# Expert products of 512 columns that walk their operands 16 bytes in every 64, in four passes

## The chip, the core and the metric

The kernel runs on one core of one Trainium2 chip. The metric is the time of one execution on the device in microseconds (us). Five engines work side by side: TensorE (PE, matrix products; its loads of stationary weights have rows of their own, PEld), VectorE (DVE), ScalarE (ACT), GpSimd (POOL) and SyncE (SP), which issues the DMAs.

## The reference

A linear attention with a decaying state runs over 4 batches, 8 heads, 768 tokens and 48 channels; its output, laid out as 3072 tokens by 384, goes through one expert (two matrix products with a gate between them):

```
for t in range(S):                       # attention, per batch and head
    cur = outer(u * k[t], v[t])
    y[t] = r[t] @ (state + cur)
    state = w[t][:, None] * state + outer(k[t], v[t])
h = x @ w_in                             # x: 3072 x 384, w_in: 384 x 2048
g = where(h >= 1, h, where(h <= -1, 0, (h + 1) ** 2 / 4))
out = g @ w_out                          # w_out: 2048 x 384
```

All of it is fp32. The expert's products are made of three terms each, high part by high part, high by low and low by high, in the 32-bit format float32r.

## The kernel before

**Tiling.** The 3072 tokens are cut into 6 blocks of 512 (`WIDE`), and the hidden width 2048 into 16 chunks `f` of 128. A *step* is one block and one chunk, and consists of `product_in`, the gate, and `product_out`:

- `product_in` makes `h` (128 hidden units by 512 tokens, one PSUM bank) out of 9 matmuls: 3 pieces `j` of the 384 inputs by 3 terms. Weights are the stationary operand (`wt`), tokens the moving one (`x`), 512 columns each.
- The gate: ACT `Relu` (L755) and `Square` (L756), DVE minimum and maximum (L757), ACT rounding to `gh` (L759), DVE remainder `gl` (L760).
- `product_out` adds into three PSUM banks `acc` with 9 matmuls, moving operand `gh` (six) or `gl` (three), 512 columns each. It runs up to two or three steps behind `product_in` (`LAG`); `h` has two buffers, `g`, `gh` and `gl` have three.

In block 0 the first 5 chunks and in block 1 the first 11 are done for each half of the block apart (`HALVES`), with 256 columns per matmul; so there are 32 half steps and 80 whole ones, 2016 expert matmuls in all, 1440 of them with 512 columns.

**Attention.** Twelve units of 256 tokens, two for each block, make the next blocks' `x` while a block runs: small matmuls (48 or 64 columns, in quarter tiles of the array: `among`, `umat`, `cross`, `along`), transposes, scans on DVE, copies on ACT. The weights arrive and are decoded during block 0. `zeros` and `warm` put matmuls on cleared data (L326) into PE's gaps in the first part.

**Order.** All operations are put into a `Plan`, which simulates the engines with the costs written beside each operation and writes out a fixed order for every engine. The order is emitted as it stands; the tile framework adds the waits on semaphores from the regions that each instruction reads and writes.

Of the kernel before, what the change touches and what calls it, by code (L numbers as in the profile page):

```python
# [32 lines left out]
WIDE = 2 * UT  # L33
# [201 lines left out]
def attention_moe(tc, a):  # L235
# [501 lines left out]
    def products(n):  # L737
# [8 lines left out]
        for half in range(2):  # L746
# [4 lines left out]
        step_ops.append(len(plan.ops))  # L751
        op("PE", 0.16 + 2.11 * k, due, [("wh", f), ("wl", f), *xs], [("b", 6 + hk)],
           lambda: product_in(nc, hs, f, x[:, 0, :, cs], x[:, 1, :, cs], w_hi, w_lo))
        c = 0.21 + 0.40 * k
        op("ACT", c, due, [("b", 6 + hk)], [("g", gk)], lambda: nc.scalar.activation(gs, hs, AF.Relu, scale=0.5, bias=0.5))  # L755
# [10 lines left out]
        for terms in LAST if done else [TERMS]:  # L766
            op("PE", 0.16 + 2.11 * k * len(terms) / 9, due, [("gh", gk), ("gl", gk), ("wh", f), ("wl", f)],
               sorted({("b", 3 + j) for _, j in terms}), fresh=begin,
               emit=lambda terms=terms: product_out(nc, [x[:, cs] for x in acc], f, ghs, gls, w_hi, w_lo, begin, end, terms))
# [64 lines left out]
def general(tc, a, ident, w_hi, w_lo):  # L834
# [65 lines left out]
    with (  # L900
# [3 lines left out]
        with tc.For_i(0, B, 1) as b:  # L904
            for third in range(UB):
                ts = slice(third * UT, third * UT + UT)
                x = sb.tile([128, 3, UT], F32, tag="x", name=f"gx{third}")
                for h in range(2):
                    for j in range(3):
                        nc.sync.dma_start(  # L910
                            out=x[64 * h : 64 * h + D, j, :],
                            in_=xd[bass.ds(b, 1), j // 2 * 2 + h, j % 2 * 64 : j % 2 * 64 + D, ts],
                        )
                        nc.sync.dma_start(
                            out=x[64 * h + D : 64 * h + 64, j, :],
                            in_=xd[bass.ds(b, 1), 2 + h, 64 + 16 * j : 80 + 16 * j, ts],
                        )
                xh = sb.tile([128, 3, UT], F32R, tag="xh", name=f"gxh{third}")
                xl = sb.tile([128, 3, UT], F32R, tag="xl", name=f"gxl{third}")
                A.copy(xh, x)  # L920
                G.tensor_tensor(out=xl, in0=x, in1=xh.bitcast(F32), op=ALU.subtract)
                o = [ps.tile([128, UT], F32, tag=f"o{j}", name=f"go{third}{j}") for j in range(3)]
                for f in range(NF):
                    hp = ps.tile([128, UT], F32, tag="h", name=f"gh{third}_{f}")
                    product_in(nc, hp, f, xh, xl, w_hi, w_lo)
                    gh, gl = gate(nc, sb, hp, f"g{third}_{f}")
                    product_out(nc, o, f, gh, gl, w_hi, w_lo, f == 0, f == NF - 1)
                for j in range(3):
                    ob = sb.tile([128, UT], F32, tag=f"ob{j}", name=f"gob{third}{j}")
                    A.copy(ob, o[j])  # L930
                    for c2 in range(2):
                        nc.sync.dma_start(out=a["out_b"][bass.ds(b, 1), third, j, :, c2], in_=ob[:, c2 * 128 : c2 * 128 + 128].rearrange("p (g s) -> p g s", g=2))


def product_in(nc, hp, f, xh, xl, w_hi, w_lo):
    n = 0
    for j in (2, 0, 1):
        cs = slice(j * 128, j * 128 + 128)
        for wx, xt in ((w_hi, xh), (w_hi, xl), (w_lo, xh)):
            nc.tensor.matmul(hp, lhsT=wx[f][:, cs], rhs=xt[:, j, :], start=n == 0, stop=n == 8)  # L940
            n += 1


# [11 lines left out]
def product_out(nc, o, f, gh, gl, w_hi, w_lo, first, stop, terms=None):  # L955
    parts = ((gh, w_hi), (gh, w_lo), (gl, w_hi))
    for i, j in terms or [(i, j) for i in range(3) for j in range(3)]:
        gt, wx = parts[i]
        cs = slice(384 + j * 128, 384 + j * 128 + 128)
        nc.tensor.matmul(  # L960
            o[j], lhsT=wx[f][:, cs], rhs=gt, start=first and i == 0, stop=stop and i == 2, skip_group_check=True
        )


# [65 lines left out]
```

## Time and profile before

| | |
|---|---|
| time, median of 3 runs | 519.95 us (519.9 to 522.65) |
| profiled execution: its span, first to last instruction | 518.1 us |
| what lies around the span, by the median | 1.85 us |
| PE busy | 501.7 us, 97% |
| PE weight loads busy (beside PE) | 413.4 us, 80% |
| DVE, ACT, POOL busy | 333.6, 296.1 and 101.0 us |
| expert matmuls, share of the chain that ended last | 69% (L940 35%, L960 34%) |
| granted TensorE clock, mean | 0.998 |

No time of the profiled execution is recorded besides its span; the median of the runs is taken for it. A matmul's record is longer than the distance between two matmuls, because they are pipelined and their ends are modelled: what a matmul costs is read from the distance between starts, not from its duration. Two times that differ by less than 0.5% (2.6 us) can't be told apart.

### The profile page before, as it was taken

Reading aid. Unit: us, or ns where it says so; the run is one execution under the profiler, and the core shown is the slowest. Engines: PE = TensorE matmul, PEld = TensorE weight load, DVE = VectorE, ACT = ScalarE, POOL = GpSimd, SP = SyncE. Lnnn points to the kernel's source line nnn. Section 1 sums busy time; section 2 is a strip of 40 time slices with the busy share of each in tenths; the row PEclk is TensorE's granted clock in tenths of the full one; section 3 lists DMA queues with packets and bytes.
Section 4 is the critical chain, followed back from the end, with each engine's and each line's share of the span. In section 5 each row is a group of like instructions: output and inputs, shape, how many; then the busy total and the mean of one; then the engine's idle time right before and its main releaser. Section 6 shows DMA issues by size and latency. Waiting matters only on the chain.

```text
span 518.1 us, 13059 instructions
## 1 busy us (share of the span) xinstructions
PE 501.7 (97%) x5558; PEld 413.4 (80%) x5558; DVE 333.6 (64%) x561; ACT 296.1 (57%) x604; POOL 101.0 (19%) x68
## 2 busy tenths in 40 slices
PE   8899999999999999999999999999999999999994
PEld 6778988788998987878788788887778888888783
DVE  6899997779986969788894476333552333433331
ACT  3578899888954656547464356443363444444441
POOL 2478767611033031111201010001000000000000
PEclk9999999999999999999999999999999999999999
DMA  8966563167624263436221240000120000100002
GB/s 319 368 231 208 207 225 121 42 217 221 208 84 146 67 210 102 152 121 211 70 105 61 77 129 1 1 1 30 40 67 1 0 1 0 62 1 0 1 0 67
DMA packets 21921, 54.11 MB, mean 104 GB/s; under 512 B 3104, under 2 KB 8672, under 8 KB 21856
## 3 DMA queue, kind: packets, MB, share of 16 engines
q1 hardware_dynamic: 21856, 53.21, 30.2%
q8 instruction: 45, 0.74, 0.6%
q14 instruction: 20, 0.16, 0.1%
HBM read 46.32 MB, written 4.72 MB: 99 GB/s over the span
## 4 chain that ended last, share of the span: by engine, by line
PE 81%; DVE 7%; ACT 4%; issue 2%; DMA 2%; POOL 1%; SPq 1%; POOLq 0%; DVEq 0%
PE h L940 35%; PE acc L960 34%; PE bank L593 4%; PE bank L483 2%; PE bank L522 2%; PE bank L544 2%; PE bank L326 1%; DMA fl<-in_w 1%; DVE g L757 1%; DVE gl L760 1%; DMA vn<-in_v 1%; SPq L692 1%; DVE y L429 1%; POOL rr L359 1%; DVE rk L513 1%
## 5 line engine op out<-in xcount | busy, mean ns | idle before, releaser
L940 PE MATMUL h<-x,wt 128*128 128x512 f32 (+1 forms) x1008 | 220.9, 366 | 2.3 <-DVE seeds L433 0.9
L940 PEld LDWEIGHTS h<-x,wt 128*128 128x128 f32 x1008 | 169.4, 188 | 35.6 <-DVE g L757 1.2
L960 PE MATMUL acc<-gh,wt 128*128 128x512 f32 (+1 forms) x672 | 155.7, 367 | 0.3 <-DVE ob L777 0.3
L960 PEld LDWEIGHTS acc<-gh,wt 128*128 128x128 f32 x672 | 113.7, 188 | 21.7 <-DVE ob L777 0.5
L757 DVE SCALAR_TENSOR_TENSOR g<-g,h 128x512 f32<-128x512 f32 (+1 forms) x112 | 67.8, 607 | 97.7 <-ACT g L756 94.6
L755 ACT ACTIVATE g<-h 128x512 f32<-128x512 f32 (+1 forms) x112 | 59.8, 534 | 85.7 <-PE h L940 80.8
L760 DVE TENSOR_TENSOR gl<-g,gh 128x512 fp32r<-128x512 f32 (+1 forms) x112 | 75.0, 672 | 37.7 <-ACT gh L759 36.6
L759 ACT CAST gh<-g 128x512 fp32r<-128x512 f32 (+1 forms) x112 | 62.2, 557 | 48.8 <-DVE g L757 48.2
L960 PE MATMUL acc<-gl,wt 128*128 128x512 f32 (+1 forms) x336 | 85.6, 363 | 0.0
L960 PEld LDWEIGHTS acc<-gl,wt 128*128 128x128 f32 x336 | 58.7, 188 | 10.8
L756 ACT ACTIVATE g<-g 128x512 f32<-128x512 f32 (+1 forms) x112 | 64.0, 571 | 3.2
L359 POOL TENSOR_SCALAR rr<-wraw 128x768 uint16<-128x768 f32 x16 | 52.8, 3302 | 34.0 <-DVE fl L361 20.9
L509 POOL TENSOR_TENSOR r<-cst,d 128x512 f32<-128x512 f32 x16 | 18.4, 1173 | 156.7 <-PE bank L593 130.9
L434 DVE TENSOR_TENSOR_SCAN p<-wq,seeds 128x514 f32<-128x514 f32 x24 | 31.4, 1308 | 3.6 <-POOL st L313 2.1
L429 DVE TENSOR_TENSOR_SCAN y<-wq,seeds 128x514 f32<-128x514 f32 x24 | 30.0, 1249 | 0.8
L501 POOL TENSOR_TENSOR nk<-nk 128x768 f32<-128x768 f32 x8 | 15.3, 1909 | 65.9 <-DMA nk<-in_nk 57.5
L529 ACT COPY kt<-bank 128x512 f32<-128x512 f32 x24 | 14.0, 582 | 13.3 <-PE bank L522 13.2
L358 ACT ACTIVATE rr<-wraw 128x768 uint16<-128x768 uint32 x16 | 17.4, 1089 | 1.2 <-DVE fl L361 0.8
L513 DVE TENSOR_TENSOR rk<-rk,p 128x512 f32<-128x512 f32 x24 | 17.7, 751 | 0.4 <-PE acc L483 0.4
L463 DVE TENSOR_TENSOR rk<-rk,y 128x512 f32<-128x512 f32 x24 | 16.4, 685 | 2.1 <-ACT nk L454 1.7
L364 DVE TENSOR_TENSOR wt<-fl,wt 128x768 fp32r<-128x768 f32 x16 | 16.1, 1004 | 2.5 <-ACT wt L351 2.1
L326 PE MATMUL bank<-clear 128*128 128x512 f32 (+1 forms) x53 | 16.1, 425 | 1.6 <-DVE seeds L433 1.6
(109 smaller groups left out, 386.6 us busy)
## 6 DMA issues: line engine op xcount, KB each, us to landing
rk<-in_rk SPq DMA_DIRECT2D x24, 512.0 KB, 5.1
wraw<-in_wbits SPq DMA_DIRECT2D x16, 768.0 KB, 7.5
wq<-in_w SPq DMA_DIRECT2D x24, 257.5 KB, 3.2
nk<-in_nk SPq DMA_DIRECT2D x8, 768.0 KB, 4.5
vn<-in_v SPq DMA_DIRECT2D x11, 384.0 KB, 6.4
fl<-in_w SPq DMA_DIRECT2D x12, 257.0 KB, 2.9
out_y<-g SPq DMA_DIRECT2D x11, 256.0 KB, 2.8
x<-last SPq DMA_DIRECT2D x66, 32.0 KB, 2.7
```

The costliest lines, as they stand in the source:

```text
L326: PE.matmul(out[:, 0 : 128 * n], lhsT=clear, rhs=clear.unsqueeze(1).broadcast_to([128, n, 128]), start=True, stop=True)
L359: op("POOL", 3.35, due, [("raw", f)], ["rr_high"], lambda: G.tensor_scalar(out=r16[:, :, 1], in0=wraw[f][:, :, 1].bitcast(F32), scalar1=0. ...
L429: V.tensor_tensor_scan(out=y_[:, ::-1], data0=w[:, SEG:0:-1], data1=sv[:, ::-1], initial=0.0, op0=ALU.mult, op1=ALU.add)
L434: V.tensor_tensor_scan(out=pv[:, q].rearrange("p n c -> p (n c)"), data0=w[:, 0:SEG], data1=sv, initial=0.0, op0=ALU.mult, op1=ALU.add,)
L513: op("DVE", 0.69, due, [("p", q)], [("r", slot[q])], lambda q=q: V.tensor_tensor(out=parts(q, 0), in0=parts(q, 0), in1=pv[:, q, :, 0:UT], ...
L755: op("ACT", c, due, [("b", 6 + hk)], [("g", gk)], lambda: nc.scalar.activation(gs, hs, AF.Relu, scale=0.5, bias=0.5))
L756: op("ACT", c, due, (), [("g", gk)], lambda: nc.scalar.activation(gs, gs, AF.Square))
L757: op("DVE", 0.13 + 0.56 * k, due, [("b", 6 + hk)], [("g", gk)], lambda: nc.vector.scalar_tensor_tensor(out=gs, in0=gs, scalar=1.0, in1=hs, ...
L759: op("ACT", c, due, [("g", gk)], [("gh", gk)], lambda: nc.scalar.copy(ghs, gs))
L760: op("DVE", 0.18 + 0.52 * k, due, [("g", gk), ("gh", gk)], [("gl", gk)], lambda: nc.vector.tensor_tensor(out=gls, in0=gs, in1=ghs.bitcast( ...
L940: nc.tensor.matmul(hp, lhsT=wx[f][:, cs], rhs=xt[:, j, :], start=n == 0, stop=n == 8)
L960: nc.tensor.matmul(o[j], lhsT=wx[f][:, cs], rhs=gt, start=first and i == 0, stop=stop and i == 2, skip_group_check=True)
```

## The change

A helper `by16` looks at the 512 columns of an operand as 32 groups (`i`) of 4 runs (`k`) of 4 fp32 numbers (`e`, 16 bytes), and walks them run by run: first run 0 of every group, then run 1, and so on. Each pass reads 16 of every 64 bytes, and four passes cover the row. The moving operand and the output in PSUM are walked the same way, so every number goes to the place it went to before, in another order of time. `product_out` uses it for every whole step, `product_in` for every whole step but those with `f` = 0. Operands of 256 columns are left as they are. So 1404 matmuls change (1440 less 4 first steps of 9), and 612 expert matmuls don't.

```diff
+def by16(t, f=1):
+    return t.rearrange("p (i k e) -> p k i e", k=4, e=4) if f and t.shape[1] == WIDE else t
+
+
 def product_in(nc, hp, f, xh, xl, w_hi, w_lo):
...
-            nc.tensor.matmul(hp, lhsT=wx[f][:, cs], rhs=xt[:, j, :], start=n == 0, stop=n == 8)
+            nc.tensor.matmul(by16(hp, f), lhsT=wx[f][:, cs], rhs=by16(xt[:, j, :], f), start=n == 0, stop=n == 8)
...
         nc.tensor.matmul(
-            o[j], lhsT=wx[f][:, cs], rhs=gt, start=first and i == 0, stop=stop and i == 2, skip_group_check=True
+            by16(o[j]), lhsT=wx[f][:, cs], rhs=by16(gt), start=first and i == 0, stop=stop and i == 2, skip_group_check=True
         )
```

No instruction changes its place on any engine, and none is added or removed but for waits. On PE, in block 0 (`h_121` and `acc_117` to `acc_119` are PSUM banks, `x_101` a block's tokens), the rows before are:

```order
L940 MATMUL h_121<-x_101,wt_1163 128x512 [waits DVE_49]
L940 MATMUL h_121<-x_101,wt_1163 128x512 x8
L960 MATMUL acc_117<-gh_109,wt_1033 128x512 [waits Activation_49]
L960 MATMUL acc_118<-gh_109,wt_1033 128x512
L960 MATMUL acc_119<-gh_109,wt_1033 128x512
```

and the rows of the changed kernel, in the same place and with the same waits:

```order
L944 MATMUL h_121<-x_101,wt_1163 128x4x32x4 [waits DVE_49]
L944 MATMUL h_121<-x_101,wt_1163 128x4x32x4 x8
L964 MATMUL acc_117<-gh_109,wt_1033 128x4x32x4 [waits Activation_49]
L964 MATMUL acc_118<-gh_109,wt_1033 128x4x32x4
L964 MATMUL acc_119<-gh_109,wt_1033 128x4x32x4
```

On DVE the framework sees the regions otherwise and moves a wait on PE's semaphore: 70 rows of L757 gain it, 48 rows of L760 lose it. From block 0, before (-) and changed (+):

```order
-L757 SCALAR_TENSOR_TENSOR g_105<-g_105,h_120 128x512 [waits Activation_49]
+L757 SCALAR_TENSOR_TENSOR g_105<-g_105,h_120 128x512 [waits PE_49,Activation_49]
 L361 SCALAR_TENSOR_TENSOR fl_114<-fl_114,rr_116 128x768 [waits Pool_49]
-L760 TENSOR_TENSOR gl_111<-g_105,gh_108 128x512 [waits PE_49,Activation_49]
+L760 TENSOR_TENSOR gl_111<-g_105,gh_108 128x512 [waits Activation_49]
```

The wait that L757 gains is for the same count of PE's semaphore as the wait of the `Relu` (L755) on the same `h`, which ACT has passed two instructions earlier. Two DMAs on SP (L692) lose a wait on PE. PE, ACT and POOL wait for what they waited for before.

## Rows read from the trace of the kernel before

**Rows 1.** The page's head: span, busy time, busy tenths in 40 slices.

```profile
span 518.1 us, 13059 instructions
...
PE 501.7 (97%) x5558; PEld 413.4 (80%) x5558; DVE 333.6 (64%) x561; ACT 296.1 (57%) x604; POOL 101.0 (19%) x68
...
PE   8899999999999999999999999999999999999994
...
PEclk9999999999999999999999999999999999999999
```

**Rows 2.** Chain of waits from 64 to 113 us and from 205 us on, by line.

```profile
by line: PE h L940 43.8%; PE acc L960 39.7%; DMA fl<-in_w 5.9%; PE bank L593 4.3%; PE bank L544 1.8%; DVE g L757 1.4%; ACT g L756 1.3%; ACT g L755 1.2%; PE bank L522 0.9%; issue 0.1%
...
by line: PE acc L960 44.8%; PE h L940 43.7%; PE bank L593 3.8%; PE bank L483 1.7%; PE bank L544 1.7%; PE bank L522 1.6%; ACT g L756 0.2%; ACT g L755 0.2%; DVE g L777 0.1%; ACT g L777 0.1%; PE bank L814 0.0%; ACT look L629 0.0%; issue 0.0%
```

**Rows 3.** Timeline of PE, two windows: start, length, then instructions merged.

```profile
266.07 2.26 PE L940 MATMUL h<-x,wt 128*128 128x512 f32 x9
268.17 1.56 PE L960 MATMUL acc<-gh,wt 128*128 128x512 f32 x6
269.57 0.86 PE L960 MATMUL acc<-gl,wt 128*128 128x512 f32 x3
270.27 2.26 PE L940 MATMUL h<-x,wt 128*128 128x512 f32 x9
...
453.79 1.56 PE L960 MATMUL acc<-gh,wt 128*128 128x512 f32 x6
455.19 0.86 PE L960 MATMUL acc<-gl,wt 128*128 128x512 f32 x3
455.88 1.56 PE L960 MATMUL acc<-gh,wt 128*128 128x512 f32 x6
457.29 0.86 PE L960 MATMUL acc<-gl,wt 128*128 128x512 f32 x3
457.99 4.36 PE L940 MATMUL h<-x,wt 128*128 128x512 f32 x18
```

**Rows 4.** Timeline of PE in a half step, 139 to 148 us: 256 columns.

```profile
143.93 1.23 PE L940 MATMUL h<-x,wt 128*128 128x256 f32 x9
144.99 0.88 PE L960 MATMUL acc<-gh,wt 128*128 128x256 f32 x6
145.71 0.51 PE L960 MATMUL acc<-gl,wt 128*128 128x256 f32 x3
146.06 1.23 PE L940 MATMUL h<-x,wt 128*128 128x256 f32 x9
```

**Rows 5.** Timeline of PE at the start: matmuls on cleared data.

```profile
6.08 1.05 PE L326 MATMUL bank<-clear 128*128 128x512 f32 x2
6.93 0.63 PE L326 MATMUL acc<-clear 128*128 128x512 f32 x1
...
8.34 1.55 PE L326 MATMUL bank<-clear 128*128 128x512 f32 x6
9.73 0.27 PE L522 MATMUL bank<-cst,rk 128*128 128x128 f32 x1
```

**Rows 6.** Busy time by stretch: us, then busy of each engine, PE clock, DMA share, GB/s.

```profile
6.00:7.35 1.35, 1.35 (x4) 0.99 (x3) 0.72 (x3) 0.06 (x1) 0.00 (x0) 1.00 1.04 386
...
64.00:113.00 49.00, 49.00 (x459) 39.47 (x458) 40.15 (x58) 42.85 (x71) 28.89 (x10) 1.00 0.39 141
113.00:181.00 68.00, 66.10 (x1081) 61.51 (x1079) 58.75 (x117) 48.57 (x130) 11.04 (x7) 1.00 0.48 152
181.00:205.00 24.00, 23.11 (x263) 18.68 (x259) 19.43 (x32) 14.05 (x32) 5.85 (x4) 1.00 0.48 157
205.00:294.00 89.00, 89.00 (x1129) 70.53 (x1131) 68.81 (x117) 48.34 (x104) 12.19 (x9) 1.00 0.34 110
294.00:369.00 75.00, 75.00 (x751) 59.85 (x744) 39.51 (x70) 36.75 (x71) 4.62 (x4) 1.00 0.13 43
439.00:506.00 67.00, 67.00 (x290) 53.68 (x289) 22.75 (x35) 30.06 (x50) 0.00 (x0) 1.00 0.03 12
```

**Rows 7.** ACT groups: reading 4 of every 8 bytes (L355), and reading without gaps (L351).

```profile
L355 ACT ACTIVATE fl<-wraw 128x768 f32<-128x768 f32 x16 | 14.5, 912 | 4.0 <-DMA wraw<-in_wbits 2.0 <-DVE wt L364 1.9
L351 ACT CAST wt<-fl 128x768 fp32r<-128x768 f32 x16 | 13.2, 825 | 3.2 <-DVE fl L361 3.1
```

**Rows 8.** Timeline of the last steps, 500 to 518 us, and the gate of the last one.

```profile
502.40 2.26 PE L940 MATMUL h<-x,wt 128*128 128x512 f32 x9
...
504.50 1.56 PE L960 MATMUL acc<-gh,wt 128*128 128x512 f32 x6
504.70 0.60 ACT L755 ACTIVATE g<-h 128x512 f32<-128x512 f32 x1 [1.12 <-PE h L940]
...
507.37 0.69 DVE L760 TENSOR_TENSOR gl<-g,gh 128x512 fp32r<-128x512 f32 x1 [0.69 <-ACT gh L759]
...
508.70 1.09 PE L960 MATMUL acc<-gh,wt 128*128 128x512 f32 x4
```

## The prediction

> **What bounds the kernel now.** I read the page's head first. PE is busy 501.7 of 518.1 us, and its tenths read 9 in nearly every slice [rows 1]; but a PE record is longer than what the matmul holds the engine for, so busy time alone proves nothing. The chain of waits does better: from 205 us to the end 88.5% of it is the two expert lines and nearly all of the rest is PE too, and from 64 to 113 us the two lines are 83.5% [rows 2]. DVE and ACT are busy for 77% and 54% of the stretch from 205 to 294 us and for 34% and 45% of the last full stretch [rows 6]. So from 205 us on the end is set by how fast PE takes one expert matmul after another, and the price of one is what the argument turns on.
>
> The timeline gives it. In the step that begins at 266.07 us the next step begins at 270.27: 4.20 us for 18 matmuls, 233.3 ns from start to start [rows 3]. At the full level of the clock, 2.4 GHz, 512 columns at one column per cycle would be 213.3 ns, and the granted clock of these stretches is 1.00 [rows 6]. So 20.0 ns of every 512-column matmul is neither clock nor columns. What is it?
>
> - Not a fixed price of an instruction: a half step takes 146.06 − 143.93 = 2.13 us for 18 matmuls of 256 columns, 118.3 ns each [rows 4]. Through the two points goes a line of 0.449 ns for a column and 3.3 ns for an instruction. So some 3 ns are fixed, and 0.449 − 0.417 = 0.033 ns for each column, 16.7 ns of the 512, grow with the length.
> - Not other engines: the distance is 4.20 us per 18 in the stretch from 205 to 294 us, where DVE is busy 77%, and also (457.99 − 453.79) in that from 439 to 506 us, where it is busy 34% [rows 3, 6].
> - Not the clock at its lower level: at the start three matmuls on cleared data begin 0.425 us apart (6.08, then two to 6.93) [rows 5], and 512 columns at 1.2 GHz are 426.7 ns, with nothing left over. The clock's row says 1.00 for that stretch [rows 6], so that this is the lower level is my reading of the distance. A little later the same instruction, six in a row, takes (9.73 − 8.34)/6 = 0.232 us [rows 5], as the expert matmuls do.
>
> So the array can take a column every cycle at the lower level and not at the higher: something that feeds or drains it gives out at about 2.2 columns per ns. That is a limit of the path of operands: the read of 4 bytes per column and partition, or the write of 4 bytes into PSUM. The matmuls on cleared data overwrite and don't accumulate, and read the same 512 bytes four times over; they run at the same rate, so neither accumulation nor the length of the row read makes the limit.
>
> **The change, part by part.** No instruction moves, PE waits for nothing new, and weights, columns and products stay as they are.
>
> *The order of the 16-byte runs.* 1404 matmuls read and write run by run at a distance of 64 bytes. No row before has a matmul that skips bytes in its moving operand or its output, so the price has to be bounded. Below: a matmul can't go under 213.3 ns at this clock, so at most 20.0 ns are saved, 1404 x 20.0 = 28.1 us. Above: the lowest rate in the trace for 512 columns, 426.7 ns [rows 5], 193.4 ns more, 272 us. Between them stand no gain at all (0, if the limit is bytes per time) and the nearest row that skips bytes on any engine: ACT takes 912 ns for 768 elements when it reads 4 of every 8 bytes, 825 without gaps [rows 7], 10.5% more with another function and output type; the same share of 233.3 is 24.6 ns, 34.5 us in all.
>
> I take a gain of the part that grows with the columns, 16.7 ns, so 216.6 ns a matmul. My reason is the shape of the limit: it lets one column through per cycle at 1.2 GHz and 0.93 of that at 2.4 GHz, for a row of 512 bytes as for one of 2048. A path just too slow in bytes would look like that, but so would a memory in which runs next to each other are served by one part that isn't ready again in time for the next run; then an order that goes to another 64 bytes with each run spreads the reads, and whole 16-byte runs are still used when they are touched. That the four numbers of a run stay together speaks against a cost like that of the ACT row, which leaves half of each piece unused.
>
> [...]
>
> *Where the saving reaches the end.* 1206 of the 1404 matmuls stand in the last five steps of block 1 and in blocks 2 to 5. 1206 x 16.7 ns = 20.1 us. The other 198 are the eleven whole steps of block 0, 3.3 us. Behind these come the half steps of block 1, where PE stands still for 1.9 of 68 us and DVE is busy 58.75 us, 86% [rows 6]; the chain of 64 to 113 us ends in a DMA piece of 5.9% [rows 2]. I count half, 1.65 us. In block 2 the stretch would fall from 89 to about 84 us with DVE's 68.8 us in it, 82%: it has room. The gate of one step takes 3.36 us, from 504.70 to 508.06 [rows 8], and is hidden by two products of 9; these fall from 4.20 to 3.90 us, still longer. After the last matmul nothing changes. Sum: 518.1 − 21.8 = 496.3 us of span; with the 1.85 us by which the median, 519.95, exceeds the span, 498.2.
>
> *The waits on DVE.* L757 now waits for a count of PE that ACT has already seen before its `Relu`, so it is passed when L757's own wait for ACT is; L760 loses the same wait. Behind L757 on DVE stand the scans and the decode, but they wait no longer than now. Nothing. If the framework had made it wait for a later product, `h` could come free about 2 us later, and PE would show new waits on L757; the count says that it didn't. The two DMAs that lose a wait can start no later than now. *What stays contiguous* keeps its price.
>
> **The rivals.**
> 1. *The limit is bytes per time.* The order of runs then doesn't matter, the distance stays 233.3 ns: 520 us. For it: the rate is the same for every row read so far, whatever the length. Against: a path that is 7% too slow for the one clock that it must serve would be odd. This is also the case in which the change does nothing that it could do.
> 2. *Slower: a jump costs.* If leaving 64 bytes behind after each 16 costs anything, there are 128 jumps in a matmul, on the read and on the write, and PE has no slack from 205 us on to hide it. At the ACT row's 10.5% the time is 520 + 34.5 = 554 us; at half rate 791. It decides from 1.9 ns per matmul (2.6 us over 1404), 15 ps per jump. For it: gaps are dearer in the one pair of rows that shows them. Against: that pair leaves half the bytes unused, this order none. [...]
> 3. *Part of the gain is lost.* Either the order removes half of the excess (8 ns, 11 us: 509), or DVE takes up everything before 294 us; then only the 837 changed matmuls of blocks 3 to 5 count, 14.0 us: 506 us. For it: DVE's 86% in the half steps and 77% in block 2. Against: PE never waits from 205 us on.
>
> **How the numbers follow.** The full gain gets 0.46: from 491 (all 28.1 us) to 502. The third rival gets 0.14, 502 to 517; the first 0.17, around 520; the second 0.23, from 523 up without a near end. Faster by over 0.5% (2.6 us, about what a measurement of this kernel can tell from no change) is 0.60, within it 0.17, slower 0.23. The range runs from 491 to 523 us and leaves the slow cases out. The likeliest case alone is 491 to 502, and its sum 498.
>
> **What the profile would show.** Right: 18 expert matmuls from start to start in about 3.90 us in blocks 2 to 5, first steps of a block with 233 ns still in `product_in`, half steps at 2.13 us as before, no new wait of PE. The first rival shows 4.20, the second more than that in the whole steps alone, and by the same factor in `product_in` and `product_out`. The third shows 4.05, or 3.90 with new idle time of PE before L940 or L960, released by DVE. I would be wrong above all if the array's path prefers neighbours: then every whole step is longer and nothing else in the profile differs.

## The result

The changed kernel takes 514.09 us (median of 4, 512.95 to 515.29), the kernel before in the same session 520.27 (519.9 to 522.65): a ratio of 0.9862, 95% interval 0.983 to 0.9895. It is faster, by 6 to 7 us, and I had forecast 22. In a later session the ratio was 0.9871 (0.9834 to 0.9908), 514.76 against 521.3 us (median of 17 runs, 519.08 to 523.69); the profiled execution of before, with 518.1 us of span and so about 519.95 us of time, lies at the low end of these.

The page of the changed kernel, head and chain:

```profile
span 513.5 us, 13078 instructions
...
PE 495.0 (96%) x5558; PEld 414.1 (81%) x5558; DVE 335.5 (65%) x561; ACT 296.4 (58%) x604; POOL 103.1 (20%) x68
...
PE acc L964 30%; PE h L944 29%; POOL rr L359 5%; PE bank L593 3%; PE bank L483 2%; DVE g L757 1%; PE bank L544 1%; PE bank L326 1%; PE bank L522 1%; DVE gl L760 1%; ACT g L756 1%; DVE fl L361 1%; DVE p L434 1%; DVE rk L463 1%; DVE rk L513 1%
```

PE is still busy nearly throughout, but the expert lines hold 59% of the chain, not 69%: other engines have come into it. What one matmul costs is in the timeline of PE, changed kernel, 266 to 272 us (start, length, instructions):

```profile
267.22 2.20 PE L944 MATMUL h<-x,wt 128*128 128x512 f32 x9
269.26 1.52 PE L964 MATMUL acc<-gh,wt 128*128 128x512 f32 x6
270.62 0.84 PE L964 MATMUL acc<-gl,wt 128*128 128x512 f32 x3
271.30 2.20 PE L944 MATMUL h<-x,wt 128*128 128x512 f32 x9
```

18 matmuls now take 4.08 us, 226.7 ns each; before they took 4.20 [rows 3]. So 6.7 of the 20.0 ns over 213.3 are gone. The 64 steps of blocks 2 to 5 carry this to the end: the first `product_in` of block 2 starts at 204.94 us before and 207.02 now, 2.08 later, and the last matmul at 510.57 and 505.40, 5.16 earlier: 7.24 us gained on the way, against 1116 x 6.67 ns = 7.4. Ahead of block 2 PE has these waits, changed kernel, 64 to 128 us (us, times, longest); before there was only one, of 0.3 us:

```profile
PE bank L522 <- DVE r L489: 2.0, 1, 2.0
PE bank L593 <- DVE st L562: 0.3, 1, 0.3
```

and in the busy times by stretch (columns as in [rows 6]):

```profile
64.00:113.00 49.00, 48.41 (x464) 39.58 (x463) 39.97 (x57) 43.74 (x73) 29.88 (x10) 1.00 0.38 132
113.00:181.00 68.00, 65.71 (x1039) 60.99 (x1038) 58.74 (x113) 46.60 (x126) 11.44 (x7) 0.97 0.50 158
205.00:294.00 89.00, 88.36 (x1099) 70.90 (x1101) 73.06 (x120) 49.91 (x107) 12.92 (x9) 1.00 0.35 110
439.00:506.00 67.00, 66.78 (x296) 54.53 (x294) 23.70 (x36) 29.69 (x50) 0.00 (x0) 1.00 0.03 12
```

Whether the change made block 2 start late is taken up under *Block 0 left out*.

### The profile page after: what moved, and what is told of

The parts are those of the page before. It is cut to its first block, busy times and chain, and to the rows that moved or that the text cites. A ratio compares the mean times of both kernels' runs of the same rounds, so it can differ in the third digit from the quotient of the medians.

```text
span 513.5 us, 13078 instructions
## 1 busy us (share of the span) xinstructions
PE 495.0 (96%) x5558; PEld 414.1 (81%) x5558; DVE 335.5 (65%) x561; ACT 296.4 (58%) x604; POOL 103.1 (20%) x68
## 4 chain that ended last, share of the span: by engine, by line
PE 70%; DVE 11%; ACT 6%; POOL 6%; issue 5%; DMA 2%; SPq 0%; POOLq 0%; DVEq 0%
PE acc L964 30%; PE h L944 29%; POOL rr L359 5%; PE bank L593 3%; PE bank L483 2%; DVE g L757 1%; PE bank L544 1%; PE bank L326 1%; PE bank L522 1%; DVE gl L760 1%; ACT g L756 1%; DVE fl L361 1%; DVE p L434 1%; DVE rk L463 1%; DVE rk L513 1%
## 5 line engine op out<-in xcount | busy, mean ns | idle before, releaser
L944 PE MATMUL h<-x,wt 128*128 128x512 f32 (+1 forms) x1008 | 216.2, 361 | 1.0 <-DMA x<-last 0.7
L964 PE MATMUL acc<-gh,wt 128*128 128x512 f32 (+1 forms) x672 | 153.1, 362 | 0.0
L757 DVE SCALAR_TENSOR_TENSOR g<-g,h 128x512 f32<-128x512 f32 (+1 forms) x112 | 67.8, 606 | 90.3 <-ACT g L756 86.3
L755 ACT ACTIVATE g<-h 128x512 f32<-128x512 f32 (+1 forms) x112 | 59.8, 534 | 79.2 <-PE h L944 73.9
L760 DVE TENSOR_TENSOR gl<-g,gh 128x512 fp32r<-128x512 f32 (+1 forms) x112 | 74.5, 667 | 36.6 <-ACT gh L759 35.6
L964 PE MATMUL acc<-gl,wt 128*128 128x512 f32 (+1 forms) x336 | 84.5, 359 | 0.0
L434 DVE TENSOR_TENSOR_SCAN p<-wq,seeds 128x514 f32<-128x514 f32 x24 | 33.0, 1373 | 4.1 <-POOL st L313 2.1
L463 DVE TENSOR_TENSOR rk<-rk,y 128x512 f32<-128x512 f32 x24 | 18.1, 755 | 5.9 <-ACT nk L454 3.1
L358 ACT ACTIVATE rr<-wraw 128x768 uint16<-128x768 uint32 x16 | 17.5, 1092 | 1.7 <-DMA wraw<-in_wbits 0.9
L593 PEld LDWEIGHTS bank<-rk,st 48*48 48x48 f32 (+1 forms) x656 | 11.5, 121 | 7.6 <-DVE st L562 2.2
```

The source lines that it names most:

```text
L434: V.tensor_tensor_scan(out=pv[:, q].rearrange("p n c -> p (n c)"), data0=w[:, 0:SEG], data1=sv, initial=0.0, op0=ALU.mult, op1=ALU.add,)
L463: op("DVE", 0.69, due, ["y"], [("k", s)], lambda q=q: V.tensor_tensor(out=parts(q, 1), in0=parts(q, 1), in1=y_.rearrange("p (n c) -> p n c ...
L593: PE.matmul(out=bank[by[g]][HP * half : HP * half + wide, lo : lo + C], start=first, stop=False, skip_group_check=True, **kw)
L757: op("DVE", 0.13 + 0.56 * k, due, [("b", 6 + hk)], [("g", gk)], lambda: nc.vector.scalar_tensor_tensor(out=gs, in0=gs, scalar=1.0, in1=hs, ...
L760: op("DVE", 0.18 + 0.52 * k, due, [("g", gk), ("gh", gk)], [("gl", gk)], lambda: nc.vector.tensor_tensor(out=gls, in0=gs, in1=ghs.bitcast( ...
L944: nc.tensor.matmul(by16(hp, f), lhsT=wx[f][:, cs], rhs=by16(xt[:, j, :], f), start=n == 0, stop=n == 8)
```

## The experiments

My theory going in: the moving operand's read is the limit, and runs next to each other are served slower than runs at a distance. The rivals: the write into PSUM is the limit; or moving reads and weight reads collide. Most kernels use the fact that blocks 2 to 5 are alike: each block gets another walk, and one trace shows four prices. Blocks 0 and 1 and each block's first `product_in` stay contiguous there. The prices below are the mean distance between the starts of consecutive expert matmuls in a block, without the shortest and longest 5%, `product_in` and `product_out` given apart where they differ. Each price comes from one execution; block 0's whole steps, contiguous there, read 233.3 or 233.4 ns in every one. In the lines that follow `C` stands for contiguous, and `both(k, e)` gives read and write the same walk: what such a block costs isn't told apart into read and write. The edit to `product_in`, against the kernel before (`product_out` is edited alike; the runs on pairs, fours and odd distances add to it):

```diff
-            nc.tensor.matmul(hp, lhsT=wx[f][:, cs], rhs=xt[:, j, :], start=n == 0, stop=n == 8)
+            nc.tensor.matmul(walk(hp, how[1]), lhsT=stay(wx[f][:, cs], how[2]), rhs=walk(xt[:, j, :], how[0]), start=n == 0, stop=n == 8)
...
+def walk(t, how):                 # how = (k, e): e numbers of every k * e, k passes
+    k, e = how
+    if k > 0:
+        return t.rearrange("p (i k e) -> p k i e", k=k, e=e)
+    if k < 0:                     # the first e numbers, again and again
+        return t[:, 0:e].unsqueeze(1).broadcast_to([128, WIDE // e, e])
+    return t
```

**Read or write.**

```diff
+PATTERNS = {2: ((4, 4), C, 0), 3: (C, (4, 4), 0), 4: ((-1, 4), C, 0), 5: ((-1, 4), (4, 4), 0)}   # read, write, weights; C contiguous
```

> Each of blocks 2 to 5 walks its operands in its own way, blocks 0 and 1 and the first product_in of a block stay contiguous; the order of the columns is no longer kept, so the output's values are not the reference's, and no work is left out. Block 2: only the moving operand is read 16 of each 64 bytes. Block 3: only PSUM is written so. Block 4: the moving operand is one 16-byte run read 128 times, PSUM contiguous. Block 5: the same read, PSUM written 16 of each 64. Read off as us for 18 matmuls from start to start (4.20 contiguous, 4.08 with both). If the read is the limit (neighbouring runs are served slower): 4.08 in block 2, 4.20 in block 3; the repeated run shows what a read of one place costs: more than 4.20 if one part of the memory must be ready again, and the same in block 5. If the write is the limit: 4.20, 4.08, 4.20, 4.08. If moving reads and weight reads collide: 4.08 in block 2, 4.20 in block 3, and in blocks 4 and 5 another value, depending on where the run lies.

Block 2 (read alone) 226.9 and 226.4 ns, block 3 (write alone) 233.2 and 233.3; one run repeated, 215.8 and 218.4, whether PSUM was written with gaps or not. Timeline of PE in this run, 18 matmuls in blocks 2, 3 and 5:

```profile
266.51 2.19 PE L959 MATMUL h<-x,wt 128*128 128x512 f32 x9
268.55 1.52 PE L981 MATMUL acc<-gh,wt 128*128 128x512 f32 x6
269.91 0.84 PE L981 MATMUL acc<-gl,wt 128*128 128x512 f32 x3
270.59 2.21 PE L959 MATMUL h<-x,wt 128*128 128x512 f32 x9
...
334.43 2.26 PE L959 MATMUL h<-x,wt 128*128 128x512 f32 x9
336.53 1.56 PE L981 MATMUL acc<-gh,wt 128*128 128x512 f32 x6
337.93 0.86 PE L981 MATMUL acc<-gl,wt 128*128 128x512 f32 x3
338.63 2.26 PE L959 MATMUL h<-x,wt 128*128 128x512 f32 x9
...
458.18 2.10 PE L959 MATMUL h<-x,wt 128*128 128x512 f32 x9
460.12 1.47 PE L981 MATMUL acc<-gh,wt 128*128 128x512 f32 x6
461.43 0.82 PE L981 MATMUL acc<-gl,wt 128*128 128x512 f32 x3
462.09 1.48 PE L981 MATMUL acc<-gh,wt 128*128 128x512 f32 x6
```

270.59 − 266.51 = 4.08, 338.63 − 334.43 = 4.20, 462.09 − 458.18 = 3.91. The write theory is out for this walk: the whole gain is the read's. And the path can take 512 columns in 215.8 and 218.4 ns, 2.5 to 5.1 over the 213.3 that 256 take at a granted clock of 0.50 (run on lengths, below), if it need not read anything new. The limit is in the reading, and not in bytes per time on the path.

**Distance.**

```diff
+PATTERNS = {2: both(2, 4), 3: both(8, 4), 4: both(16, 4), 5: both(32, 4)}   # 16 bytes of each 32, 128, 256, 512
```

> Runs of 16 bytes, read and written at another distance in each block: 32 bytes in block 2, 128 in block 3, 256 in block 4, 512 in block 5; blocks 0 and 1 contiguous; the output is the reference's. If neighbouring runs share one part of the memory, a larger distance gives at least what 64 bytes give: 4.08 us or less for 18 matmuls in blocks 3 to 5, and 32 bytes something between 4.08 and 4.20. If the reads collide with the weight reads by their place, distances have no order: some above and some below 4.08. If the write sets it, the same order is seen as with the read, and the run on sides tells them apart.

233.1, 246.3, 276.6 and 266.7 ns. PE's timeline in this run, block 4, nine matmuls at 256 bytes:

```profile
408.51 1.82 PE L981 MATMUL acc<-gh,wt 128*128 128x512 f32 x6
410.17 1.00 PE L981 MATMUL acc<-gl,wt 128*128 128x512 f32 x3
411.00 1.27 PE L959 MATMUL h<-x,wt 128*128 128x512 f32 x4
```

411.00 − 408.51 = 2.49 us for 9, 276.7 ns each. Only 64 bytes (226.6) gain; each of the three larger distances costs more than no distance at all, up to 43 ns. "Spreading helps" fails here: spreading more makes it worse.

**Length of a run.**

```diff
+PATTERNS = {2: both(8, 2), 3: both(4, 8), 4: both(4, 16), 5: both(2, 2)}   # 8 of 64, 32 of 128, 64 of 256, 8 of 16
```

> Another length of run in each block, read and written alike: block 2 8 of each 64 bytes, block 3 32 of each 128, block 4 64 of each 256, block 5 8 of each 16; blocks 0 and 1 contiguous; the output is the reference's. If a 16-byte run is the unit and neighbours are served slower: longer runs have neighbours again, so block 3 lies between 4.08 and 4.20 (about 4.14) and block 4 near 4.17; runs of 8 bytes touch each unit twice and are slower than 4.20 for 18 matmuls. If reads collide with weight reads: block 2 and 5 slower too, blocks 3 and 4 without order.

431.3, 227.9, 238.4 and 453.3 ns. Runs of 8 bytes take nearly twice the time: a step of 18 in block 2 (PE's timeline in this run) begins at 300.97 and ends at 308.73, 7.76 us:

```profile
300.97 4.06 PE L959 MATMUL h<-x,wt 128*128 128x512 f32 x9
304.85 2.77 PE L981 MATMUL acc<-gh,wt 128*128 128x512 f32 x6
307.44 1.47 PE L981 MATMUL acc<-gl,wt 128*128 128x512 f32 x3
308.73 0.61 PE L959 MATMUL h<-x,wt 128*128 128x512 f32 x1
```

For each run that is 431.3 / 256 = 1.68 ns with 8 bytes; the 16-byte runs of the changed kernel take 226.7 / 128 = 1.77, and every 16 bytes of the contiguous row 1.82. This would fit a read that costs nearly the same for 8 bytes as for 16. Four columns take 1.67 ns at 213.3 for 512 (an estimate, worked out below), so a run could just be brought in time, and whatever holds one up would not be made good: a reader without reserve is the picture that I missed. It is not shown: PSUM was written in runs of 8 bytes too, and no run tries the 8-byte read or write alone. 64 of each 256 bytes (238.4 ns, 4.29 us for 18) came out slower than contiguous, where I had expected about 4.17. Nor do whole runs of 16 bytes ensure the contiguous price: read alone, 96 bytes apart, they took 319.9 ns (below).

The same run shows beside a recorded clock what the prediction could only take from a distance between starts: with the doubled clock a matmul's time is not halved. Its blocks 0 and 1 are contiguous, and for a while in block 0 the granted clock is 0.50 (busy times as in [rows 6], then PE's timeline):

```profile
54.20:57.40 3.20, 3.20 (x17) 3.20 (x16) 1.98 (x4) 2.79 (x7) 2.91 (x1) 0.50 0.98 320
56.14 1.47 PE L981 MATMUL acc<-gh,wt 128*128 128x256 f32 x6
57.42 0.43 PE L981 MATMUL acc<-gl,wt 128*128 128x256 f32 x2
```

(57.42 − 56.14)/6 = 213.3 ns for 256 columns; at 1.00 they take 118.3 [rows 4], 11.6 more than half of that. In the changed kernel 512 columns take (123.87 − 123.02)/2 = 0.425 us in a stretch at 0.50 (122.20 to 125.50 us, shown under *Block 0 left out*):

```profile
123.02 1.05 PE L964 MATMUL acc<-gh,wt 128*128 128x512 f32 x2
123.87 1.48 PE L964 MATMUL acc<-gl,wt 128*128 128x512 f32 x3
```

No row and no run gives a clock in GHz or columns per cycle. What is shown of the 2.4 GHz in my prediction is 1.2 columns per ns at a granted clock of 0.50; twice that is its 213.3 ns for 512 columns, an estimate, and the excess of 20.0 ns is counted from there.

**Weights from one place.** The same walks with `lhsT` one column broadcast to 128, so that weight loads touch one run.

```diff
+    return w[:, 0:1].broadcast_to([128, 128]) if how else w
...
+PATTERNS = {2: (C, C, 1), 3: ((4, 4), (4, 4), 1), 4: ((-1, 4), C, 1), 5: ((-1, 4), (4, 4), 1)}
```

> In blocks 2 to 5 all 128 columns of the weights are read from one place (the first column), so that weight loads touch one 16-byte run only; the products are then not the reference's, the amount of work is kept. Block 2: moving operand and PSUM contiguous. Block 3: both 16 of each 64 bytes. Block 4: moving operand one run repeated, PSUM contiguous. Block 5: the same, PSUM 16 of each 64. If the limit is the moving operand's own read: 4.20 us for 18 in block 2, 4.08 in block 3, as with real weights. If the moving reads collide with the weight reads: less than 4.20 in block 2, down to 3.90 (216.6 ns each), and about the same in block 3. If PSUM's write sets the rate: 4.20 in blocks 2 and 4, 4.08 in 3 and 5.

231.5 and 232.0 contiguous, 223.6 and 225.5 at 64 bytes, 215.7 and 218.1 for one run, as with real weights. Reading the weights from one place takes off 1 to 3 ns of the 17.5 to 20; if that is the two reads colliding, it is a small part of the limit.

**Pieces read again and again.**

```diff
+PATTERNS = {2: ((-1, 8), C, 0), 3: ((-1, 16), C, 0), 4: ((-1, 64), C, 0), 5: ((-1, 128), C, 0)}   # 32, 64, 256, 512 bytes
```

> Reads alone are changed, PSUM is written contiguous and weights are the real ones; values are not the reference's, the amount of work is kept. The moving operand is a piece of the row read again and again until 512 columns are full: 32 bytes in block 2, 64 in block 3, 256 in block 4, 512 in block 5. One run of 16 bytes repeated took 3.88 to 3.93 us for 18 matmuls, the whole row of 2048 takes 4.20. If the step from a run to its neighbour is what costs, 32 bytes are already near 4.20 and all longer pieces too. If it is a larger unit that has to be changed, short pieces stay near 3.9 and the excess comes with the length at which the unit is left: at 64, 256 or 512 bytes. If collisions with weight reads made it, the value would depend on the place and have no order.

215.9 and 218.7 for 32 bytes, 243.3 for 64, 233.4 for 256 and for 512. Two runs are as good as one, four are worse than the whole row.

**Two runs, and four runs, in turn at a distance.** Both kernels differ in the piece repeated; `product_in` and `product_out` have distances of their own.

```diff
+        return t[:, 0 : 2 * d].rearrange("p (a d) -> p a d", a=2)[:, :, 0:4].unsqueeze(1).broadcast_to([128, 64, 2, 4])   # four: 4 * d, a=4, 32
```

> In blocks 2 to 5 every moving operand is just two 16-byte runs read in turn, 64 times each; the values are not the reference's, the amount of work is kept, PSUM is contiguous. product_in reads runs that lie 32 bytes apart in block 2, 64 in block 3, 128 in block 4, 256 in block 5; product_out 512, 1024, 48 and 96 bytes. Two runs next to each other (16 bytes apart, in the run on spans) took 3.89 and 3.94 us for 18, as one run did, and 64 bytes repeated took 4.38. If a part of the memory serves 32 bytes at a time and has to be ready again before it serves another 32, every distance here costs, and the distances at which both runs are in the same part cost most (well above 4.4); distances whose runs are in different parts cost nothing, 3.89 to 3.94. If the cost comes from leaving a run at all, all eight are alike. If it comes from the length of the row touched, all eight are near 3.9.

Two runs: 216.0 to 216.5 in `product_in` and 218.2 to 219.0 in `product_out` at all eight distances, that is nothing beyond one run repeated (215.8 and 218.4).

> As in the run on pairs, but four 16-byte runs are read in turn, 32 times each; values are not the reference's, the amount of work is kept. product_in reads runs 32 bytes apart in block 2, 64 in block 3, 128 in block 4, 256 in block 5; product_out 512, 80, 48 and 96 bytes apart. Four neighbours (64 bytes repeated) took 4.38 us for 18, two runs at any distance 3.89 to 3.94. If two runs are kept and every third has to be fetched, all eight pay for fetches, 4.0 us or more; and if fetches collide by their distance, the order is that of the full rows: 48 and 64 bytes least (near 4.1), then 32, 128, 80, and 96, 256 and 512 most (4.8 or more). If fetches don't collide with each other but with something else, all eight are alike.

Four runs: 238.2, 234.8, 258.5 and 287.0 ns at 32, 64, 128 and 256 bytes, 287.0, 238.1, 243.6 and 244.4 at 512, 80, 48 and 96. PE's timeline in the run on four, block 2, where `product_in` reads at 32 bytes and `product_out` at 512:

```profile
267.70 2.30 PE L962 MATMUL h<-x,wt 128*128 128x512 f32 x9
269.84 1.88 PE L984 MATMUL acc<-gh,wt 128*128 128x512 f32 x6
271.56 1.03 PE L984 MATMUL acc<-gl,wt 128*128 128x512 f32 x3
272.42 2.31 PE L962 MATMUL h<-x,wt 128*128 128x512 f32 x9
```

269.84 − 267.70 = 2.14 us for 9 at 32 bytes, 272.42 − 269.84 = 2.58 at 512. These runs change the read alone, so the read's price depends on distance by itself. I read it so: two runs are kept, with four there is always one to be brought, and its price depends on where the others lie; a keeping of runs is argued, not shown. 64 bytes are the best here too, and 256 and 512, with the same price, the worst. The full rows follow this at 32 to 256 bytes, but not everywhere (below), so I don't claim to know the rule.

**Other orders.** Runs that alternate between far parts of the row (`"p (k i e) -> p i k e"`), longer runs, and single passes at odd distances out of a larger tile:

```diff
+PATTERNS = {2: both(102, 4), 3: both(104, 4), 4: both(102, 8), 5: both(108, 4)}   # 100 + k: k parts of the row in turn
+PATTERNS = {2: both(2, 8), 3: both(8, 8), 4: both(2, 16), 5: both(2, 32)}         # 32 of 64, 32 of 256, 64 of 128, 128 of 256
+    return flat[:, 0 : how[0] * 128].rearrange("p (i s) -> p i s", s=how[0])[:, :, 0:4]   # product_in alone: s = 12, 20, 24, 16
```

> The output is the reference's. Consecutive runs lie far apart and alternate between parts of the row: block 2 runs of 16 bytes alternating between the two halves of 1024 bytes, block 3 between four quarters of 512 bytes, block 4 runs of 32 bytes between two halves, block 5 runs of 16 bytes between eight parts of 256 bytes. A fixed distance of 64 bytes took 4.08 us for 18, of 128, 256 and 512 bytes 4.43, 4.98 and 4.80. If large distances as such cost, all are above 4.3, and block 4 lies between block 2 and 4.20. If it is the fixed place of consecutive runs in a period of 256 or 512 bytes that costs (the same part of the memory again), blocks 2, 3 and 5 are the worst, near 4.8 to 5.0, as all their steps are multiples of 256. If spreading alone helped, as I forecast, they would be at or below 4.08.

253.3, 266.7, 242.2 and 277.0 ns: the order is that of "large distances as such cost" (4.56, 4.80, 4.36 and 4.99 us for 18: all above 4.3, block 4 between block 2 and 4.20). It doesn't single out a period of 256 bytes: block 2 misses the 4.8 said for that, and the step back to the first part is 16 bytes off a multiple. Two halves taken in turn, 1024 bytes apart, cost 20 ns (253.3 against 233.4) although each half is read in order.

> The output is the reference's. Longer runs at other distances: block 2 32 of each 64 bytes, block 3 32 of each 256, block 4 64 of each 128, block 5 128 of each 256. 32 of 128 took 4.10 us for 18, 64 of 256 4.29, contiguous 4.20. If the distance of 64 bytes is what helps, block 2, which steps 16 and 48 in turn, lies at 4.1 to 4.2; if 64-byte units alternate, block 4, which steps from every second unit to the next, gains something: 4.1. Block 3 with its 240-byte steps should lie above 4.3, block 5 at 4.20 to 4.25.

233.2, 247.1, 240.0 and 233.3 ns. No order of longer runs beats 16 of 64 bytes, and block 4, 64 of 128, loses 7 ns where I had expected a gain.

> In blocks 2 to 5 product_in (but the first of a block) reads 128 runs of 16 bytes at one fixed distance in a single pass, out of the whole of the tokens' tile: 48 bytes apart in block 2, 80 in block 3, 96 in block 4, 64 in block 5. It multiplies other tokens than the reference asks for, with the same number of columns; PSUM and product_out are contiguous, so product_out stays at 4.20 us for 18. If the four passes matter (the turns back), 64 bytes in one pass differs from 4.08: near 3.9 if the turns are what is left. If the distance alone sets it, block 5 reads 4.08. If parts of the memory alternate in powers of two, distances of 48 and 80 bytes visit all of them in turn and give the least, 3.88 to 4.0; 96 lies near 32 bytes' 4.20. If only neighbours matter, as I first thought, all four are 4.08 or less.

226.6 ns at 48 bytes, 266.6 at 80, 319.9 at 96, and 237.0 at 64 in one pass over four times the length (226.7 in four passes over the row). So the distance alone doesn't set the price. The length that is walked grows with the distance here, from 6144 bytes (48) to 12288 (96), and is not told apart from it. Odd distances don't remove the excess, so a memory whose parts simply alternate in powers of two is not it. Of some 25 orders none with the real weights came under 226 ns but those that read one or two runs.

**Block 0 left out.**

```diff
+PATTERNS = {b: both(4, 4) for b in (2, 3, 4, 5)}
```

> The changed kernel with blocks 0 and 1 left contiguous; blocks 2 to 5 as in the change, first steps contiguous. The output is the reference's. 1116 matmuls are changed, by 6.67 ns each: 7.4 us. If the changed kernel's late start of block 2 (2.08 us later than before) is the luck of that execution, this one is 7.4 us faster than before, ratio 0.986, the changed kernel another 1.9 us at best. If the faster matmuls of block 0 upset the first part (PE comes earlier to work that DVE has not ready), this one is as fast as or faster than the changed kernel: 0.983 to 0.986.

514.75 us, ratio 0.9879 (0.982 to 0.9938). And the changed kernel once more, unaltered, in a later session:

> The changed kernel once more, for the size of its gain beside the other runs: 36 first-step products apart, 1404 x 6.67 ns = 9.4 us at most; 64 steps of blocks 2 to 5 give 7.4 us in the trace. Ratio to the kernel before between 0.982 and 0.989, and the profiled execution shows whether block 2 begins later than before (by 2.08 us in the first profile) or earlier (by up to 1.9 us): later again means that the change costs the first part something.

514.76 us, ratio 0.9871 (0.9834 to 0.9908). The 288 matmuls of blocks 0 and 1, up to 1.9 us, make no difference that shows. Block 2's second `product_in` starts at 214.73 us before, 216.68 and 216.37 in the two profiles of the changed kernel and 216.79 without block 0. But the start of block 2 varies by itself: in the eleven runs of this document that leave blocks 0 and 1 as they were, its first `product_in` begins between 203.01 and 207.67 us, and 204.94 (before), 207.02 and 206.70 (changed) all lie inside. Neither a gain of 1.9 us nor a loss of that size can be told there from one or two profiles. From block 2 on the gain repeats: 7.24, 7.15 (second profile) and 7.47 us (without block 0).

About 1 us of the lateness is there before any changed matmul runs: the first expert matmul begins at 28.20 us before, at 29.21 and 29.44 in the changed kernel, at 29.50 without block 0. That goes with the granted clock. From 18.40 to 24.00 us it is 1.00 before and 0.70 in the changed kernel's first profile, where it drops once more, to 0.50, 1 us after the end of the wait of 2.0 us shown above. Before, then changed, first profile (busy times as in [rows 6]):

```profile
18.40:24.00 5.60, 5.18 (x107) 4.71 (x108) 4.14 (x6) 3.10 (x9) 2.52 (x2) 1.00 1.03 356
...
18.40:24.00 5.60, 5.56 (x99) 5.06 (x91) 3.77 (x6) 2.09 (x6) 2.93 (x2) 0.70 1.04 380
122.20:125.50 3.30, 3.30 (x20) 2.17 (x21) 2.86 (x5) 2.53 (x7) 0.00 (x0) 0.50 0.39 87
```

In all fifteen profiles the first expert matmul begins at 27.46 to 28.39 us in the four whose clock stays full around there (1.00 before, above), and at 29.21 to 29.50 in the eleven in which it drops (to 0.70 in the changed kernel, above), changed or not.

From 64 to 128 us the kernel that leaves block 0 alone has no wait of PE at all; the changed kernel had those shown above, and in its second profile these:

```profile
PE bank L544 <- ACT kt L529: 1.0, 1, 1.0
PE acc L964 <- DVE ob L777: 0.6, 1, 0.6
PE bank L522 <- DVE r L489: 0.4, 1, 0.4
PE bank L593 <- DVE st L562: 0.4, 1, 0.4
```

These are 2.3 and 2.4 us of waiting for DVE and ACT. The eleven runs with the old blocks 0 and 1 have 0 to 1.9 us there, up to 1.6 of it for the same L489, so at most some half a microsecond sets the changed kernel apart. The step that begins at 92.88 us before is 0.36 us less late in the changed kernel than the first whole step was, and the next one, at 101.66, has lost it again (0.91, 0.55, 1.02 us late).

**Half steps too.**

```diff
-    return t.rearrange("p (i k e) -> p k i e", k=4, e=4) if f and t.shape[1] == WIDE else t
+    return t.rearrange("p (i k e) -> p k i e", k=4, e=4) if f else t
```

> The changed kernel with the half steps (256 columns, all but those of the first chunk) walked in the same way, 16 of each 64 bytes; the output is the reference's. 630 fewer... of the 576 matmuls of half steps 504 change (28 half steps by 18), with product_out of the first chunks 540. If the saving grows with the columns, each gains 3.3 ns: 1.8 us in sum at most. But in block 1 the early half steps then wait for DMAs of the other half's tokens. If these waits cost more than 1.8 us, the time is above the changed kernel's 514.1; if not, down to 512.3. I expect no difference that can be told, 512 to 516.

524.01 us, ratio 1.0056 (1.0033 to 1.008): slower than the kernel before. The matmuls of block 1's half steps do gain, 118.3 to 114.6 ns on average. But PE now waits for DMAs of tokens in the middle of the half steps (before: one wait of 0.8 us). The longest wait stands before a chunk whose own tokens five chunks have read already; as my expectation says, these are the other half's, and the likely reason is that the framework takes a walk with gaps for more than one half, which the profile can't show. Waits of PE in this run:

```profile
PE h L944 <- DMA x<-last: 7.9, 3, 4.7
```

and the busy times around the longest of them (columns as in [rows 6]):

```profile
142.00:148.80 6.80, 5.26 (x23) 5.06 (x23) 3.19 (x6) 2.93 (x8) 0.00 (x0) 0.50 0.08 17
```

From 3 us into that wait of 4.7 us on, the granted clock is 0.50 for 6.8 us, and block 2 starts 11 us later than before. I had expected no difference.

## Why the prediction was right and wrong

- *What bounds the kernel, and where 20 ns per matmul go: right.* Neither the clock's lower level nor other engines nor a fixed price; a limit of the operands' path that shows at a granted clock of 1.00, where 256 columns take 118.3 ns, 11.6 over half of what they take at 0.50. The recorded clock of the run on lengths bears out the lower level that I had read from a distance: 0.50, and 213.3 ns for 256 columns there. The runs narrow the limit to the read of the moving operand.
- *The order of the 16-byte runs: the mechanism had the right sign, and this is the step that failed, by its size.* I took all of the 16.7 ns that grow with the columns (216.6 ns a matmul); 6.7 went, to 226.7. The reason I gave, that going to another 64 bytes with each run spreads the reads, would have made larger distances as good; they are worse than contiguous. 16 of 64 bytes is one of the few orders found that cost less; it keeps two thirds of the excess. That one part "isn't ready again in time" is not shown by any run; one 16-byte run read over and over, which that should hurt most, takes 215.8. Nor is it shown that 16 bytes are a unit of the read. With 6.67 ns the sum reads 1206 x 6.67 = 8.0 us for the late part, and 7.24 were found from block 2 on.
- *Half of block 0's gain: too much.* I counted 1.65 of 3.3 us; at 6.67 ns it would be 0.66 of 1.3, and none was found, in a stretch whose end varies by 4.7 us without the change. That DVE takes up what is gained there, the third rival's mechanism, is possible and not shown; from 205 us on nothing is lost (1116 x 6.67 = 7.4, found 7.24).
- *Third rival: the nearest.* "The order removes half of the excess", 8 ns and 509 us, against 6.7 ns and 514. I gave it 0.14.
- *First rival, bytes per time: wrong.* One run repeated has the same bytes per time through the array and takes 215.8 ns.
- *Second rival, slower: wrong for this walk, right for its neighbours.* 16 of 128, 256 or 512 bytes, read and written so, cost 13, 43 and 33 ns a matmul. The write of this walk costs nothing that shows: writing 16 of each 64 bytes alone left 233.2 ns, and with a repeated read 215.8 either way. No other walk was written alone.
- *The waits on DVE: right.* No wait of PE names L757 in the changed kernel, and DVE's idle time before L757 fell from 97.0 to 89.7 us. Two of these waits (0.6 and 0.5 us) are put down to PE, but both times L757 starts 0.03 us after the `Square` before it ended, as it does in the kernel before.

## What to carry over

When a matmul's time isn't halved as the granted clock doubles (here 213.3 ns for 256 columns at 0.50, 118.3 at 1.00), ask which operand path has no reserve, and test read and write apart: a kernel whose equal blocks each try another access pattern prices four of them in one run. A mechanism that explains an excess doesn't say how much of it a change takes away; without a row for the new pattern, put the likeliest value inside the bounds, not at the end of one. And a gain of 1 or 2 us in a stretch that varies by more between executions needs many of them, or a place behind it from which to count.

## What was not expected of the hardware

- Runs of 8 bytes, read and written so, cost a matmul nearly twice its time (431 and 453 ns for 512 columns, against 233). Whether the read or the write does it was not tried.
- One or two 16-byte runs of the moving operand read over and over cost next to nothing beyond the 213.3 ns estimated above (215.8 to 219.0 ns, two at any of the distances tried, 16 to 1024 bytes); four cost 234.8 to 287.0, by their distance, worst at 256 and 512 bytes. Which runs hold each other up stays open, and so does why 48 bytes in one pass and 64 in four (226.6) beat 16, 32, 80, 96 and 64 in one pass (237.0).
- PSUM can be written 16 of every 64 bytes, in four passes, without a loss that shows: 233.2 and 233.3 ns, against 233.3 or 233.4 contiguous.
